# The second feed-forward layer of 28 token blocks as seven quarter products per group of four, with their variance on ScalarE

## The chip, the core and the metric

The kernel runs on one core of a Trainium2 chip. The metric is the device time of one execution in microseconds, from the first to the last instruction. Five engines work side by side, each with its own queue: TensorE (PE in the profile; its weight loads are PEld), VectorE (DVE), ScalarE (ACT), GpSimd (POOL), which here issues the loads of the inputs, and SyncE (SP), which issues the stores and the transposing transfers.

## The reference

The inputs are q, k and v (8 batches, 8 heads, 576 tokens, 64 per head), a gain g of 512 and two weight matrices of 512x2048 and 2048x512, all float32.

```
scores = q k^T / 8, with a bias -slope_h * |i - j|; only 0 <= i - j < 128 is seen
attn   = softmax(scores) v
x      = attn with its heads side by side: (8, 576, 512)
xn     = (x - mean(x)) / sqrt(var(x) + 1e-6) * g
out    = x + relu(xn @ w_ch1) @ w_ch2
```

## The kernel before

**Blocks.** The 4608 tokens are cut into 36 blocks of 128: four pairs of batches, nine blocks each; the ninth (number T = 8 of its pair) holds the last 64 tokens of both batches. The text numbers blocks 0 to 35 in the order of work.

**Attention of a block** is a list of steps written out by hand. From block 8 on there are two to a block. The first (called the *big step* here) takes the masked weights of the block times v into two PSUM tiles `ps_pv` (`values`, L430), divides them on DVE by the sums (L438, L439), centres x to float16 `xc` (`centre`, L459 and L478), lets SP transpose it by DMA into the group's `xT` (L488), computes the scores of the block after next (`scores`, L382, with the exponent on ACT, L390), and in some steps turns the q and k of a later pair of blocks: on PE through two tiles `ps_tr` and copies on DVE and ACT (`turn`, L269, L288 to L294), or for later blocks with a transposing DMA on SP (`turn_natural`, L302). The second (the *mask step*) multiplies the exponents with the decay mask on DVE (L401, two instructions).

**The feed-forward part** works on groups of blocks, `GROUPS = [2] * 4 + [3] * 4 + [4] * 4`. `mlp1(g)` makes the 16 slices of the hidden layer: for each, four matmuls (L636) with a slice of w1 as weights and all columns of the group's `xT` (256, 384 or 512) as the moving operand, then a ReLU to float16, on ACT (L652) or for a few slices on DVE (L644). `mlp2(g)` takes each block by itself: 16 matmuls of 512 columns (L666) with the hidden slice as weights and w2 as the moving operand, all into one PSUM tile, and then one DVE instruction (`finish`, L682) that multiplies with `rstd`, adds x and gives the float32 output, which SP stores with two DMAs (L694, L698). The variance is `bn_stats` and `bn_aggr` on DVE (L503, L504), one block after another in the odd units of `mlp1`, and `inv_std` (L512 to L530) follows for the whole group.

**The order.** `weave_at` (L700) runs the units of `mlp1` or `mlp2` and puts the next attention step behind the units that its list names; -1 is before the first unit. A unit is one slice of `mlp1` (four matmuls) or two matmuls of `mlp2`. PE, ACT and DVE follow the program text exactly, each in order. SP and POOL are ordered by a planner, which goes by its own costs; their queues too are worked off in order. So a matmul stands behind everything that the text puts ahead of it on PE, and a wait of one instruction holds all that follows on its engine.

**PSUM.** The scores have two tiles of two banks each. All else (`ps_m` of both layers, `ps_pv`, `ps_tr`) shares the pool `ps_mm`: four tiles of one bank. A new tile waits until the readers of an old one are done.

The main loop before:

```
            weave_at(mlp2(3), -1, -1, 7, 7)
            for g in range(4, len(GROUPS)):
                in_first = g in (6, 8, 9, 10)
                weave_at(mlp1(g, (9,) * in_first), *(8, 10) * in_first, group=g)
                places = [-1, 7, 15] if g < 8 else [-1, 15, 23] if g < 10 else [-1, 7]
                weave_at(mlp2(g), *2 * places)
```

So in the last groups of three the big steps stand ahead of each block of `mlp2`; in `mlp2(7)`, for instance, those of blocks 22, 23 and 24, while `mlp1(8)` needs blocks 20 to 23.

Of the kernel before, what the change touches and what calls it, by code (L numbers as in the profile page):

```python
# [10 lines left out]
FP16 = mybir.dt.float16  # L11
# [6 lines left out]
P = 128  # L18
# [4 lines left out]
T = 8  # L23
NSLOT = 9
HALF = P // 2
GROUPS = [2] * 4 + [3] * 4 + [4] * 4

NV = 10
AHEAD = 6
# [1 line left out]
FIRST_GROUPS, FIRST = 2, 4  # L31

BY_DMA = SEEN = 8

TURN_BY_DMA = 22

# [23 lines left out]
def kernel(  # L60
# [21 lines left out]
    def pool(name, bufs, **kw):  # L82
        return ctx.enter_context(tc.tile_pool(name=name, bufs=bufs, **kw))
# [30 lines left out]
    def decay(m, at):  # L114
# [340 lines left out]
    def centre(p, blk):  # L455

        total = sums.pop((p, blk))
        mean = small.tile([P, 1], FP32, tag="mean", name="mean")
        nc.vector.tensor_scalar(  # L459
            out=mean,  # L460
            in0=total[:, 0:1],
            scalar1=total[:, 1:2],
            scalar2=1.0 / DM,
            op0=ALU.add,
            op1=ALU.mult,
        )
# [14 lines left out]
        n = p * NSLOT + blk  # L481
        g, at = home[n]
        if at == 0:
            turned_x[g] = group_pool.tile([P, NKB, 4 * P], FP16, tag="xT", name="xT")
        if n < BY_DMA:
            centred[p, blk] = xc
        else:
            nc.sync.dma_start_transpose(  # L488
                out=turned_x[g][:, :, at * P : (at + 1) * P], in_=xc
            )  # L490
# [12 lines left out]
        nc.vector.bn_stats(out=st, in_=xs[order[n]])  # L503
        nc.vector.bn_aggr(out=moments[:, n, :], in_=st)  # L504

    def inv_std(first, n):
# [5 lines left out]
        nc.vector.tensor_scalar(  # L512
            out=aa, in0=moments[:, blocks, 1], scalar1=EPS, scalar2=None, op0=ALU.add
        )
# [51 lines left out]
    def masks_of(n, *halves):  # L566
        return [(masks,) + order[n] + halves]
# [33 lines left out]
    for n in range(8, count):  # L601
        first_half, second_half = values_steps(n)
        step = first_half + second_half
        if n + 1 < count and order[n + 1][1] == T:
            step += [(scores_tail, order[n][0])]
        if n + 2 < count:
            step += scores_step(n + 2)
        if n + 3 < count and order[n + 3][1] % 2 == 0 and not by_dma(*order[n + 3]):
            step += turn_step(n + 3)
        for tag, m in (("k", n + 5), ("q", n + 4)):  # L610
            if m < count and order[m][1] % 2 == 0 and by_dma(*order[m]):
                p, blk = order[m]
# [15 lines left out]
    def mlp1(g, on_dve=()):  # L628
        xT = turned_x[g]
        w = w1 if g < FIRST_GROUPS else w1g  # L630
        cols = len(members[g]) * P
        ht = hidden[g] = hidden_pool.tile([P, NFB, 4 * P], FP16, tag="ht", name="ht")
        for fb in range(NFB):
            ps = ps_mm.tile([P, 4 * P], FP32, tag="mm", name="ps_m1")
            for kb in range(NKB):
# [6 lines left out]
                )  # L642
            if fb in on_dve:
                nc.vector.tensor_scalar(  # L644
                    out=ht[:, fb, 0:cols],
                    in0=ps[:, 0:cols],
                    scalar1=0.0,
                    scalar2=None,
                    op0=ALU.max,
                )  # L650
            else:
                nc.scalar.activation(  # L652
                    out=ht[:, fb, 0:cols], in_=ps[:, 0:cols], func=AF.Relu
                )
            yield cols

    def mlp2(g, parts=((0, NFB),)):
# [3 lines left out]
        for first, end in parts:  # L661
            for at, (p, blk) in enumerate(members[g]):
# [12 lines left out]
                if end == NFB:  # L675
                    finish(p, blk, sums[at])
                    yield DM

    def finish(p, blk, ps):
        n = p * NSLOT + blk  # L680
        o = out_pool.tile([P, DM], FP32, tag="o", name="o")
# [5 lines left out]
            op0=ALU.mult,  # L687
            op1=ALU.add,
        )
        for b, t0, w, p0 in spans(p, blk):  # L690
            dst, src = out[b, t0 : t0 + w, :], o[p0 : p0 + w, :]
            if blk == T:
                last = p == NPAIR - 1 and b % 2 == 1
                (nc.scalar if last else nc.sync).dma_start(out=dst, in_=src)  # L694
# [2 lines left out]
                for r in range(2):  # L697
                    nc.sync.dma_start(out=dst[r], in_=src[r * HALF : (r + 1) * HALF])  # L698

    def weave_at(units, *places, group=None):  # L700


        size = len(members[group]) if group else 0
        first = sum(GROUPS[:group])
# [18 lines left out]
    with tc.manual_schedule(engines={engine.PE}):  # L723
        with tc.manual_schedule(engines={engine.Activation, engine.DVE}):
# [46 lines left out]
```

## Time and profile before

| what | value |
|---|---|
| median of 3 runs | 321.09 us (319.6 to 321.68) |
| the profiled execution's own time | 321.68 us |
| its span | 321.7 us (nothing lies around it) |
| mean granted TensorE clock | 0.994 |
| PE busy | 310.8 us, 97% |
| DVE busy | 198.1 us, 62% |
| ACT busy | 179.4 us, 56% |
| POOL busy | 103.6 us, 32% |
| matmuls of the second layer (L666) | 576, 40% of the chain that ended last |
| matmuls of the first layer (L636) | 768, 40% of that chain |

The profile is of one execution. The chain that ended last is followed back from the last instruction to what released each step. A matmul's duration in the list of groups contains the time of its passage through the array, so a row of matmuls takes less than their number times that duration: what one costs in a row is read from the chain's stretches. Idle time before an instruction is put down to what released it last.

### The profile page before, as it was taken

How to read it: one execution, taken by the hardware profiler on the slowest of the kernel's cores; microseconds unless marked ns; L12 is line 12 of the kernel's file. 1: busy time of each engine (PE TensorE's matmuls, PEld its weight loads, DVE VectorE, ACT ScalarE, POOL GpSimd, SP SyncE). 2: the span in 40 equal slices, each digit the busy share in tenths (PEclk: the TensorE clock that was granted, in tenths of full speed). 3: DMA queues.
4: the chain of work that ended last, by engine and by line, in shares of the span. 5: the costliest groups of instructions: out<-in, count | busy, mean ns of one | idle time of the engine just before them, and what ended most of it. 6: DMA issues, size and time to landing. Idle time of an engine off the chain costs nothing.

```text
span 321.7 us, 9136 instructions
## 1 busy us (share of the span) xinstructions
PE 310.8 (97%) x3806; PEld 177.1 (55%) x3806; DVE 198.1 (62%) x621; ACT 179.4 (56%) x304; POOL 103.6 (32%) x144
## 2 busy tenths in 40 slices
PE   8889999999999999999999989999999999999994
PEld 3478655858656556556556633555455645544441
DVE  2688878787882782877673785437844784516011
ACT  6588756767757557648637634734473457206500
POOL 8933678567311660572680323120000000000000
PEclk9999999999999999999999997999999999999999
DMA  9999999999990993999999599994302320151032
GB/s 117 170 206 195 193 138 192 196 145 140 111 143 0 129 152 51 95 135 153 148 190 141 51 133 144 148 107 91 70 18 43 83 59 19 42 92 33 0 67 65
DMA packets 127260, 35.41 MB, mean 110 GB/s; under 512 B 118385, under 2 KB 122609, under 8 KB 127218
## 3 DMA queue, kind: packets, MB, share of 16 engines
q0 software_dynamic: 92352, 18.36, 72.4%
q1 hardware_dynamic: 34786, 16.33, 29.1%
q8 instruction: 30, 0.49, 0.7%
q14 instruction: 12, 0.10, 0.1%
q10 hardware_dynamic: 80, 0.13, 0.1%
HBM read 36.90 MB, written 9.44 MB: 144 GB/s over the span
## 4 chain that ended last, share of the span: by engine, by line
PE 92%; POOL 2%; DMA 2%; ACT 1%; DVE 1%; issue 1%; POOLq 0%
PE ps_m L666 40%; PE ps_m L636 40%; PE ps_pv L430 5%; PE ps_sc L382 5%; DMA k<-in_k_dram 2%; PE ps_tr L269 2%; POOL q L186 1%; POOL k L186 1%; ACT probs L390 1%; PE ps_sc L269 1%; POOL vx L214 1%; PE ps_tx L498 0%; DVE o L682 0%; ACT k L289 0%; ACT q L288 0%
## 5 line engine op out<-in xcount | busy, mean ns | idle before, releaser
L666 PE MATMUL ps_m<-w,ht 128*128 128x512 f16 x576 | 131.2, 380 | 0.0
L652 ACT ACTIVATE ht<-ps_m 128x384 f16<-128x384 f32 (+2 forms) x183 | 89.8, 491 | 64.7 <-PE ps_m L636 62.0
L636 PE MATMUL ps_m<-xT,w1g 128*128 128x512 f16 (+2 forms) x640 | 116.0, 340 | 2.2 <-DVE st L503 2.2
L636 PEld LDWEIGHTS <-w1g 128*128 128x128 f16 x640 | 62.3, 98 | 52.3 <-issue 4.9
L666 PEld LDWEIGHTS <-ht 128*128 128x128 f16 x576 | 53.4, 98 | 60.7
L390 ACT ACTIVATE probs<-ps_sc 128x1024 f16<-128x1024 f32 x56 | 54.2, 1027 | 43.0 <-PE ps_sc L382 42.8
L682 DVE SCALAR_TENSOR_TENSOR o<-ps_m,rstd,x 128x512 f32<-128x512 f32 x36 | 26.9, 748 | 51.3 <-PE ps_m L666 51.3
L214 POOL DMA_DIRECT2D vx<-in_v_dram x40 | 34.0, 858 | 70.6 <-PE ps_pv L430 41.6
L438 DVE RECIPROCAL rec<-ps_pv 128x4 f32<-128x4 f32 x72 | 12.8, 178 | 44.5 <-PE ps_pv L430 44.4
L401 DVE TENSOR_TENSOR probs<-probs,m 128x1024 f16<-128x1024 f16 x56 | 36.3, 683 | 2.3 <-ACT probs L390 2.1
L439 DVE SCALAR_TENSOR_TENSOR x<-ps_pv,rec 128x256 f16<-128x256 f32 x72 | 30.5, 424 | 2.5
L186 POOL DMA_DIRECT2D q<-in_q_dram x28 | 18.9, 681 | 21.3 <-DMA q<-q 7.8
L503 DVE BATCH_NORM_STATS2 st<-x 128x6 f32<-128x512 f16 x36 | 24.1, 668 | 0.0
L430 PEld LDWEIGHTS <-probs 128*128 128x128 f16 x448 | 18.7, 97 | 6.3 <-DVE probs L401 0.3
L382 PE MATMUL ps_sc<-q,k 64*64 64x128 f16 (+1 forms) x1088 | 19.8, 208 | 1.4 <-ACT probs L390 1.0
L186 POOL DMA_DIRECT2D k<-in_k_dram x28 | 18.6, 676 | 4.9 <-DMA w<-in_moe_w_ch_dram 3.2
L430 PE MATMUL ps_pv<-vx,probs 128*128 128x65 f16 x448 | 20.1, 193 | 0.0
L203 POOL DMA_DIRECT2D q<-in_q_dram x24 | 16.6, 723 | 8.7 <-issue 8.7
L382 PEld LDWEIGHTS <-k 64*64 64x64 f16 x1088 | 14.4, 107 | 6.4 <-issue 4.2
L390 ACT ACTIVATE own<-ps_sc 128x1024 f16<-128x1024 f32 x12 | 11.9, 1030 | 7.3 <-PE ps_sc L382 7.3
L636 PE MATMUL ps_m<-xT,w 128*128 128x256 f16 x128 | 15.0, 273 | 0.0
L636 PEld LDWEIGHTS <-w 128*128 128x128 f16 x128 | 12.1, 98 | 1.3
(59 smaller groups left out, 186.7 us busy)
## 6 DMA issues: line engine op xcount, KB each, us to landing
out_dram<-o SPq DMA_DIRECT2D x71, 128.0 KB, 3.3
k<-in_k_dram POOLq DMA_DIRECT2D x32, 128.0 KB, 6.2
vx<-in_v_dram POOLq DMA_DIRECT2D x32, 128.0 KB, 6.5
w<-in_moe_w_ch_dram POOLq DMA_DIRECT2D x8, 512.0 KB, 10.0
q<-in_q_dram POOLq DMA_DIRECT2D x20, 128.0 KB, 5.6
q<-in_q_dram POOLq DMA_DIRECT2D x32, 64.0 KB, 5.0
k<-in_k_dram POOLq DMA_DIRECT2D x8, 64.0 KB, 4.7
vx<-in_v_dram POOLq DMA_DIRECT2D x8, 64.0 KB, 4.4
```

The costliest lines, as they stand in the source:

```text
L186: nc.gpsimd.dma_start(out=t[b * n // 2 : (b + 1) * n // 2], in_=src[2 * p + b, :, i * P : i * P + n, :].rearrange("h (c r) d -> c h r d", ...
L214: nc.gpsimd.dma_start(out=vx[p0 : p0 + n, :, 0:D], in_=v[b, :, t0 : t0 + n, :].rearrange("h p d -> p h d"),)
L382: nc.tensor.matmul(in_halves(ps[cols, j, n, t, :])[:, r, queries], kt[rows, hp, cols], in_halves(qt[rows, b, hp])[:, r, queries], start=Tr ...
L390: nc.scalar.activation(out=dst.rearrange("p (n j) q -> p j n q", j=2), in_=ps.rearrange("p j n t q -> p j n (t q)"), func=AF.Exp, scale=in ...
L401: nc.vector.tensor_tensor(out=dst, in0=dst, in1=mask, op=ALU.mult)
L430: nc.tensor.matmul(ps[:, i, :], pr[:, h, t, :], vext[(p * NSLOT + o) % NV][:, h, :], start=(n == 0), stop=(n == len(terms) - 1),)
L439: nc.vector.scalar_tensor_tensor(out=xs[p, blk][:, hg * 4 * D : (hg + 1) * 4 * D].rearrange("p (h d) -> p h d", h=4), in0=ps[:, :, 0:D], s ...
L503: nc.vector.bn_stats(out=st, in_=xs[order[n]])
L636: nc.tensor.matmul(ps[:, 0:cols], w[:, kb, fb * P : (fb + 1) * P], xT[:, kb, 0:cols], start=(kb == 0), stop=(kb == NKB - 1),)
L652: nc.scalar.activation(out=ht[:, fb, 0:cols], in_=ps[:, 0:cols], func=AF.Relu)
L666: nc.tensor.matmul(sums[at], ht[:, fb, at * P : (at + 1) * P], w2[:, fb, :], start=(fb == 0), stop=(fb == NFB - 1),)
L682: nc.vector.scalar_tensor_tensor(out=o, in0=ps, scalar=rstd[:, n : n + 1], in1=xs[p, blk], op0=ALU.mult, op1=ALU.add,)
```

## The change

- The last 28 blocks form seven groups of four (blocks 8 to 11, 12 to 15, and so on), where there were four groups of three and four of four.
- For these groups the product of the hidden layer (512 tokens x 2048) with w2 (2048 x 512) is taken in quarters: A11, A12, A21, A22 are 256 tokens x 1024, B11 to B22 are 1024 x 256. Seven products of such quarters (Winograd's form of Strassen's scheme) replace eight. A product is 2 x 8 matmuls with a moving operand of 256 columns (`product`).
- The sums of quarters of w2 (t1 to t4) are made once, by eight DVE instructions in `mlp1(3)` and `mlp2(3)`, in the memory of w1, which only the first two groups use. The sums of quarters of the hidden layer (S1 to S4) are made for each group, by eight DVE instructions of 128x1024 float16: five among the units 5, 9, 12 and 13 of `mlp1`, three at its end.
- The results of the products are added on DVE by `onto`, two instructions of 128x256 for each product, fourteen for a group. Two PSUM tiles go on accumulating: x takes products 1, 3, 5 and 7, and `onto` reads it after each; y takes products 4 and 6; t takes product 2. With P1 to P7 in the order of the text, P3 writes x after `onto` of P1 has read it, P5 after that of P3, P7 after that of P5, and P6 writes y after that of P4.
- Each half row of a block's output is stored by itself: 16 stores for a group in place of 8.
- The variance of these blocks comes from a Square with an accumulated sum on ACT (`square`), in the mask step, in place of `bn_stats` and `bn_aggr`; `inv_std` divides by 512.
- The hidden layer has one buffer (`ht_all`) in place of two.
- `mlp1` of each of the first six of these groups takes a big step at unit 8 and a mask step at unit 10; `mlp2_seven` has 28 units, four to a product, and takes a big step before P1, behind P2 and behind P4, and a mask step behind P1, P3 and P5. The last group takes none. So the big step of the last block that `mlp1(g + 1)` needs stands behind P4 of group g, and that of block 11 still stands in the middle of `mlp2(3)`, where `mlp1(4)` now needs it.

```
--- before.py
+++ after.py
-GROUPS = [2] * 4 + [3] * 4 + [4] * 4
+GROUPS = [2] * 4 + [4] * 7
...
+SEVEN = 4
...
-    xc_pool = pool("xc", 4)
+    xc_pool = pool("xc", 5)
...
-    hidden_pool = pool("hidden", 2)
-    out_pool = pool("outp", 4)
+    out_pool = pool("outp", 5)
+    sums_pool = pool("sums", 1)
...
+    w2sums = w1.rearrange("p kb (n d) -> p (kb n) d", d=DM // 2).rearrange(
+        "p (t fb) d -> p t fb d", t=4
+    )
...
+    ht_all = consts.tile([P, NFB, 4 * P], FP16)
...
-        if n < BY_DMA:
+        if n < BY_DMA or g >= SEVEN:
             centred[p, blk] = xc
-        else:
+        if n >= BY_DMA:
             nc.sync.dma_start_transpose(
                 out=turned_x[g][:, :, at * P : (at + 1) * P], in_=xc
             )
...
+    def square(n):
+        junk = sums_pool.tile([P, DM], FP16, tag="junk", name="junk")
+        nc.scalar.activation(
+            out=junk,
+            in_=centred.pop(order[n]),
+            func=AF.Square,
+            accum_out=moments[:, n, 1:2],
+        )
...
-        steps.append([m for t in (n + 1, n + 2) if t < count for m in masks_of(t)])
+        step = [m for t in (n + 1, n + 2) if t < count for m in masks_of(t)]
+        steps.append(step + [(square, n)] * (home[n][0] >= SEVEN))
...
-        ht = hidden[g] = hidden_pool.tile([P, NFB, 4 * P], FP16, tag="ht", name="ht")
+        at = g % 2 * cols if len(members[g]) == 2 else 0
+        ht = hidden[g] = ht_all[:, :, at : at + cols]
...
+    half = NFB // 2
+    left, right = slice(0, DM // 2), slice(DM // 2, DM)
+    b11, b12 = w2[:, 0:half, left], w2[:, 0:half, right]
+    b21, b22 = w2[:, half:NFB, left], w2[:, half:NFB, right]
+    t1, t2, t3, t4 = (w2sums[:, i] for i in range(4))
+    def minus(out, a, b, op=ALU.subtract):
+        nc.vector.tensor_tensor(out=out, in0=a, in1=b, op=op)
+    def sum_w2(i):
+        c = slice(4 * (i // 4), 4 * (i // 4) + 4)
+        out, a, b = [(t1, b12, b11), (t3, b22, b12), (t2, b22, t1), (t4, b21, t2)][i % 4]
+        minus(out[:, c], a[:, c], b[:, c])
+    hsums = {}
+    def sum_hidden(g, i, c):
+        ht = hidden[g]
+        mid = ht.shape[2] // 2
+        a11, a21 = ht[:, 0:half, 0:mid], ht[:, 0:half, mid:]
+        a12, a22 = ht[:, half:NFB, 0:mid], ht[:, half:NFB, mid:]
+        if (g, i) not in hsums:
+            hsums[g, i] = sums_pool.tile([P, half, mid], FP16, tag=f"s{i}", name=f"s{i}")
+        s = hsums[g, i]
+        c = slice(4 * c, 4 * c + 4)
+        if i == 1:
+            minus(s[:, c], a21[:, c], a22[:, c], ALU.add)
+        elif i == 2:
+            minus(s[:, c], hsums[g, 1][:, c], a11[:, c])
+        elif i == 3:
+            minus(s[:, c], a11[:, c], a21[:, c])
+        else:
+            minus(s[:, c], a12[:, c], hsums[g, 2][:, c])
+    def mlp2_seven(g):
+        ht = hidden[g]
+        s = [hsums.pop((g, i)) for i in (1, 2, 3, 4)]
+        a11, a12, a22 = ht[:, 0:half], ht[:, half:NFB], ht[:, half:NFB]
+        def product(ps, lhs, off, rhs, first):
+            for pair in range(2):
+                at = off + pair * P
+                for fb in range(half):
+                    nc.tensor.matmul(
+                        ps[:, pair, :],
+                        lhs[:, fb, at : at + P],
+                        rhs[:, fb, :],
+                        start=(first and pair == 0 and fb == 0),
+                        stop=(fb == half - 1),
+                        skip_group_check=True,
+                    )
+                    if fb % 4 == 3 and not (pair == 1 and fb == half - 1):
+                        yield
+        def onto(ps, blocks, cols, o=None):
+            fresh = o is None
+            if fresh:
+                o = out_pool.tile([P, 2, DM // 2], FP32, tag="o", name="o")
+            for pair in range(2):
+                p, blk = members[g][2 * blocks + pair]
+                n = p * NSLOT + blk
+                nc.vector.scalar_tensor_tensor(
+                    out=o[:, pair],
+                    in0=ps[:, pair],
+                    scalar=rstd[:, n : n + 1],
+                    in1=xs[p, blk][:, cols] if fresh else o[:, pair],
+                    op0=ALU.mult,
+                    op1=ALU.add,
+                )
+            return o
+        def leave(o, blocks, cols):
+            for pair in range(2):
+                store(*members[g][2 * blocks + pair], o[:, pair], cols)
+        def bank2():
+            t = ps_mm.tile([P, DM], FP32, tag="mm", name="ps_s")
+            return t.rearrange("p (r d) -> p r d", r=2)
+        top, low = 0, 1
+        x = bank2()
+        yield from product(x, a11, 0, b11, True)
+        o11 = onto(x, top, left)
+        yield
+        t = bank2()
+        yield from product(t, a12, 0, b21, True)
+        onto(t, top, left, o11)
+        leave(o11, top, left)
+        yield
+        yield from product(x, s[1], 0, t2, False)
+        o12 = onto(x, top, right)
+        yield
+        y = bank2()
+        yield from product(y, s[0], 0, t1, True)
+        o22 = onto(y, low, right)
+        yield
+        yield from product(x, s[2], 0, t3, False)
+        onto(x, low, right, o22)
+        leave(o22, low, right)
+        yield
+        yield from product(y, s[3], 0, b22, False)
+        onto(y, top, right, o12)
+        leave(o12, top, right)
+        yield
+        yield from product(x, a22, 2 * P, t4, False)
+        leave(onto(x, low, left), low, left)
+        yield
...
-    def weave_at(units, *places, group=None):
+    def weave_at(units, *places, seven=None, sums=None):
...
-            if u % 2 and u // 2 < size:
-                variance(first + u // 2)
-                if u // 2 == size - 1:
-                    inv_std(first, size)
+            if seven is not None:
+                if u == 1:
+                    blocks = len(members[seven])
+                    inv_std(sum(GROUPS[:seven]), blocks, 1.0 / DM)
+                for i, c in {5: [(3, 0)], 9: [(3, 1)], 12: [(1, 0), (2, 0)], 13: [(4, 0)]}.get(u, []):
+                    sum_hidden(seven, i, c)
+                if u == NFB - 1:
+                    for i in (1, 2, 4):
+                        sum_hidden(seven, i, 1)
+            if sums is not None and u % 4 == 1:
+                sum_w2(sums + u // 4)
             advance_to(done + places.count(u))
...
-            weave_at(mlp1(3, (9, 10, 11)), 8, 12)
-            weave_at(mlp2(3), -1, -1, 7, 7)
+            weave_at(mlp1(3, (9, 10, 11)), 8, 12, sums=0)
+            weave_at(mlp2(3), -1, -1, 7, 7, sums=4)
             for g in range(4, len(GROUPS)):
-                in_first = g in (6, 8, 9, 10)
-                weave_at(mlp1(g, (9,) * in_first), *(8, 10) * in_first, group=g)
-                places = [-1, 7, 15] if g < 8 else [-1, 15, 23] if g < 10 else [-1, 7]
-                weave_at(mlp2(g), *2 * places)
+                ahead = g + 1 < len(GROUPS)
+                weave_at(mlp1(g, (9,) * ahead), *(8, 10) * ahead, seven=g)
+                weave_at(mlp2_seven(g), *[-1, 3, 7, 11, 15, 19] * ahead)
```

More of the change, by code (lines that the diff above doesn't have):

```diff
@@ L504, in variance, with inv_std @@
         nc.vector.bn_aggr(out=moments[:, n, :], in_=st)
-    def inv_std(first, n):
+    def square(n):
[6 more added lines that the diff above has]
+        )
+    def inv_std(first, n, scale=None):
         blocks = slice(first, first + n)
@@ L511, in inv_std @@
         hh = small.tile([P, 4], FP32, tag="hh", name="hh")[:, 0:n]
-        nc.vector.tensor_scalar(
-            out=aa, in0=moments[:, blocks, 1], scalar1=EPS, scalar2=None, op0=ALU.add
-        )
+        if scale is None:
+            nc.vector.tensor_scalar(
+                out=aa, in0=moments[:, blocks, 1], scalar1=EPS, scalar2=None, op0=ALU.add
+            )
+        else:
+            nc.vector.tensor_scalar(
+                out=aa,
+                in0=moments[:, blocks, 1],
+                scalar1=scale,
+                scalar2=EPS,
+                op0=ALU.mult,
+                op1=ALU.add,
+            )
         nc.vector.tensor_scalar(
@@ L644, in mlp1 @@
                 nc.vector.tensor_scalar(
-                    out=ht[:, fb, 0:cols],
+                    out=ht[:, fb, :],
                     in0=ps[:, 0:cols],
@@ L652, in mlp1 @@
                 nc.scalar.activation(
-                    out=ht[:, fb, 0:cols], in_=ps[:, 0:cols], func=AF.Relu
+                    out=ht[:, fb, :], in_=ps[:, 0:cols], func=AF.Relu
                 )
@@ new lines @@
+    hsums = {}
[14 more added lines that the diff above has]
+            minus(s[:, c], a11[:, c], a21[:, c])
+        else:
+            minus(s[:, c], a12[:, c], hsums[g, 2][:, c])
@@ new lines, in mlp2_seven @@
+    def mlp2_seven(g):
[13 more added lines that the diff above has]
+                        skip_group_check=True,
+                    )
+                    if fb % 4 == 3 and not (pair == 1 and fb == half - 1):
[12 more added lines that the diff above has]
+                    in1=xs[p, blk][:, cols] if fresh else o[:, pair],
+                    op0=ALU.mult,
+                    op1=ALU.add,
+                )
+            return o
[33 more added lines that the diff above has]
+        yield
@@ L689, in finish, with store @@
         )
+        store(p, blk, o)
+    def store(p, blk, o, cols=slice(0, DM)):
         for b, t0, w, p0 in spans(p, blk):
-            dst, src = out[b, t0 : t0 + w, :], o[p0 : p0 + w, :]
+            dst, src = out[b, t0 : t0 + w, cols], o[p0 : p0 + w, :]
             if blk == T:
@@ L698, in finish @@
                     nc.sync.dma_start(out=dst[r], in_=src[r * HALF : (r + 1) * HALF])
-    def weave_at(units, *places, group=None):
-        size = len(members[group]) if group else 0
-        first = sum(GROUPS[:group])
+    def weave_at(units, *places, seven=None, sums=None):
         advance_to(done + places.count(-1))
         for u, _ in enumerate(units):
-            if u % 2 and u // 2 < size:
-                variance(first + u // 2)
-                if u // 2 == size - 1:
-                    inv_std(first, size)
+            if seven is not None:
[9 more added lines that the diff above has]
+                sum_w2(sums + u // 4)
             advance_to(done + places.count(u))
```

## The prediction

> **What bounds the kernel now.** The page first: busy times and the chain that ended last.
>
> ```profile
> PE 310.8 (97%) x3806; PEld 177.1 (55%) x3806; DVE 198.1 (62%) x621; ACT 179.4 (56%) x304; POOL 103.6 (32%) x144
> ...
> PE 92%; POOL 2%; DMA 2%; ACT 1%; DVE 1%; issue 1%; POOLq 0%
> ```
>
> TensorE is the bound, and after the first 20 us almost without a gap. The second view is that chain in order of time (start, us, what):
>
> ```profile
> 79.71 3.17 PE ps_m L636 x28
> ...
> 88.48 0.46 PE ps_sc L382 x16
> 88.95 3.57 PE ps_m L666 x16
> 92.52 10.40 PE ps_m L636 x64
> ...
> 188.00 3.57 PE ps_m L666 x16
> ...
> 193.72 9.62 PE ps_m L636 x36
> ...
> 289.65 13.81 PE ps_m L636 x64
> 303.46 13.83 PE ps_m L666 x64
> ```
>
> A matmul of 512 columns costs 13.81/64 = 0.216 us in a row, one of 384 costs 0.1625, one of 256 costs 0.109 (28 in 3.17, less the 0.11 by which sixteen of 512 exceed 16 x 0.216 when they begin after other work). Half the columns is half the price: the weight load of each is covered. The one hole stands at the start of `mlp1(8)`: 191.57 to 193.72, and after it 36 matmuls take 9.62 instead of 7.77. The waits and the stretch after the hole (PE, PEld, DVE, ACT and POOL busy, PEclk, DMA share, GB/s):
>
> ```profile
> PE ps_m L636 <- DVE st L503: 2.2, 1, 2.2
> ```
>
> ```profile
> 194.90:198.40 3.50, 3.50 (x10) 1.22 (x8) 2.44 (x11) 1.57 (x3) 2.55 (x4) 0.51 0.86 110
> ```
>
> The named DVE instruction is a neighbour in time: what landed at 193.62 is the transposed `xT` of block 23, whose `xc` was done at 184.66. So a late `xT` cost 2.15 us of waiting and 1.85 us of half clock. The third view is that transfer, from its issue:
>
> ```profile
> L488 SPq DMA_TRANSPOSE xT<-xc x28: 1188/1275/1859, 74.4 to 281.1; - x28
> ...
> DMA to landing us min/median/max: 2.4/4.6/8.1
> ```
>
> Cut to windows: 4.6 for block 11, 5.6 for block 15, 8.1 for 23, 2.4 for most after 225 us, when the loads have ended. Last, the rows of DVE that I price with:
>
> ```profile
> L401 DVE TENSOR_TENSOR probs<-probs,m 128x1024 f16<-128x1024 f16 x56 | 36.3, 683 | 2.3 <-ACT probs L390 2.1
> L439 DVE SCALAR_TENSOR_TENSOR x<-ps_pv,rec 128x256 f16<-128x256 f32 x72 | 30.5, 424 | 2.5
> L682 DVE SCALAR_TENSOR_TENSOR o<-ps_m,rstd,x 128x512 f32<-128x512 f32 x36 | 26.9, 748 | 51.3 <-PE ps_m L666 51.3
> L503 DVE BATCH_NORM_STATS2 st<-x 128x6 f32<-128x512 f16 x36 | 24.1, 668 | 0.0
> ```
>
> **TensorE's own work.** Removed: 28 x 16 = 448 matmuls of 512, 448 x 0.216 = 96.8 us. Added: 7 x 7 x 16 = 784 of 256, 784 x 0.109 = 85.5. That is -11.3. The first layer: 256 of 384 and 256 of 512 (41.6 + 55.3) become 448 of 512 (96.8), -0.1. The hole of block 23 is taken out whole, -4.0, and late `xT` are counted anew below. The end: 4.39 us now lie between the last matmul and the end. After the change two `onto` (0.84) replace one `finish` (0.75), and SP issues three half stores, 0.47 to 0.6 each, where it issued one: +0.3. Base: 321.7 - 11.3 - 0.1 - 4.0 + 0.3 = 306.6 us.
>
> **DVE in the product phase.** Per group leave: four variances, 3.3 us (192.27 to 195.58), and four `finish`, 3.0. Come: eight sums like L401, some 0.65 each in a row, 5.2; fourteen `onto` like L439, 0.42 each, 5.9. So +4.8 or so, to about 26 us in a group of about 30 (four big steps 7.0, four mask steps 5.2, `inv_std` 2.1, a ReLU 0.7 beside the two above). That alone would be cover enough, but it is bunched. From the end of `mlp1` to the end of P7, DVE has three sums (1.95), three big steps (rec to `xc` 1.75 each), three mask steps (1.29 each) and fourteen `onto` (5.9): 17 us. TensorE has 7 x 1.75 + 3 x 0.95 = 15.1. And it is bound to DVE by x and y. The queue of one group without `turn` on PE, in us after the last matmul of `mlp1`; the last ReLU (0.60) ends at 0.65, a `ps_pv` pair with its scores takes 0.95:
>
> ```
> DVE: sums 0.65-2.60 | big 2.60-4.35 | onto P1 -5.19 | mask -6.48 | onto P2 -7.32
>      big -9.07 | onto P3 -9.91 | mask -11.20 | onto P4 -12.04 | big -13.79 (xc)
>      onto P5 -14.63 | mask -15.92 | onto P6 -16.76 | onto P7 -17.60
> PE:  big 0-0.95 | P1 -2.70 | P2 -4.45 | big -5.40 | P3 -7.15
>      P4 7.32-9.07 (its tile y: t is free at 7.32) | big -10.02 | P5 -11.77
>      P6 12.04-13.79 (onto P4) | P7 14.63-16.38 (onto P5)
> ```
>
> 16.38 against 15.10: +1.3 for a group. Where a big step also turns q and k on PE, two more of the four `ps_mm` tiles are wanted while x, t or y are held: `turn` waits until DVE has read t and the `ps_pv`. Behind P2 that is 7.32 and 7.9, so P3 starts at 8.2 instead of 5.4; behind P4 it is 12.6 and 13.2, so P5 starts at 13.5 instead of 10.0. Worked to the end: the group of blocks 8 to 11 (a turn at both places) +3.7, that of 16 to 19 (one behind P4) +3.4. Sum: 3.7 + 3.4 + 4 x 1.3 = 12.3; the last group has no attention and no such wait (P1 and P2 cover the sums). Bounds: 0 if DVE's order leaves cover that I don't see; 18 if each of the some 25 instructions of the phase takes 0.04 more, the gap between L438's end and L439's start in this trace, +1 a group. The Squares on ACT (near L652's 0.60, four to a group, 2.4) lie beside ReLUs and exponents, 17 us of 30: nothing; `inv_std` waits for the last of them, done before P7. The one buffer of the hidden layer costs nothing either: PE reads group g to its end before it makes the first slice of g + 1. The eight sums of w2 stand where DVE waits 0.94 for block 6's last matmul: nothing, or up to 0.7 on block 11.
>
> **Late `xT`.** `mlp1(4)` used to need blocks 8 to 10. Now it needs block 11: `xc` ready at 90.55, landed at 95.25, against 92.5: +2.75, the surest term. In the later groups the last block's `xc` is ready at 13.79 above and P7 ends at 16.38: a lead of 2.6, where block 23 had 6.9. While loads run a transpose needs 5.6: the next `mlp1` waits to 19.4, +3.0 (block 19). After a `turn`, where P7 is late already, +0.65 (blocks 15 and 23). Block 27 (4.9): +2.3. Block 31 (2.4): 0. Block 35 (2.4 to 3.8): +0.7, as no scores follow it. Sum 10.1. Bounds: 3 (block 11 alone) and 20 (8.1 instead of 5.6 for three blocks, and SP behind: blocks 18 and 19 were issued 4.7 and 3.3 us after their `xc`, behind q and k transposes; the stores, now 16 of 0.55 to a group, stand in that queue too).
>
> **Half clock.** Three of these waits (blocks 11, 19, 27) are longer than the 2.15 that was followed by half clock. I take half of them, at 1.85: +2.8; bounds 0 and six, 11. The Trainium skill, page TensorE: Matmul & The Clock Gate, section "What's actually happening", has the clock fall after at least one idle window of about 3.4 us. By that no wait of my list would be long enough and the sum would be 329.0; this trace differs, with a clock of 0.51 after 2.15 us of idling.
>
> **The sum.** 306.6 + 12.3 + 10.1 + 2.8 = 331.8: I predict 332 us, 3.2% above the 321.7 of the profile, 3.4% above the median of 321.09.
>
> **Rivals.**
> 1. *The removed columns win.* If DVE keeps up (the table's lateness falls under half, 6) and transposes land in 2.4 to 4 us, as they do after 225 us, so that only block 11 waits: 306.6 + 6 + 2.75 = 315.4; with a lateness of 2, 311. For it: DVE's total of 26 us in 30 fits, and each `onto` has one product as cover. Against it: 17 us against 15.1 between `mlp1` and P7, and loads run to 216 us.
> 2. *Even.* The same with 2 or 3 waits of 3 us and one half clock: 318 to 324. It lies between.
> 3. *SP's queue becomes the bound.* In the groups of blocks 16 to 27 SP has, per 30 us, 16 stores (8.8), four x transposes (5.1) and some eight q and k transposes (10): 24 us, in order, with waits for loads and DVE. If x transposes are issued 5 us late, as around block 18, three waits grow by 5 and each brings half clock: 332 + 15 + 3 = 350. For it: block 24's transpose was issued 10.9 us after its `xc`. Against it: a stalled TensorE also slows what fills the queue.
> 4. *The change does not remove what it says:* a matmul of 256 with weights from the sums at a price over 0.109, say the 0.1625 of 384 columns: 784 x 0.053 = 42 us more. The 256-wide rows of `mlp1` have a fresh weight for each too, so I give this 0.01 within the third.
>
> **Chances and range.** Forecast 0.58 (324.5 to 342), first rival 0.23 (308 to 318), second 0.11, third 0.08. A difference of 1% is about what this measurement can tell from none. Faster 0.23, same 0.11, slower 0.66. The range 311 to 343 leaves out the slow rival (0.08), the lower part of the fast one (0.07) and little of the forecast.
>
> **What would show it.** PE busy falls by some 11 us less what the clock adds. The list of waits gets PE `ps_m` at L636 on something of SP or a neighbour, once for most groups, the first at about 92.5 for 2.75 us; PE `ps_s` waits on DVE `o`, about 1 us a group; `ps_tr` waits on DVE in three places. DVE rises to about 235 us (198.1 + 7 x 4.8 + eight sums of w2). The granted clock dips after the first of them. The last group takes 26.0 us from its first matmul to its last, instead of 27.6: if that is not so, the price of 256 columns was wrong. I am wrong if TensorE runs through the starts of `mlp1`: then transposes were faster than 5.6 us, or the planner put them ahead on SP.

## The result, and the profile after

| | before | after |
|---|---|---|
| median | 321.07 us (319.6 to 321.68, 4 runs) | 343.47 us (341.89 to 346.04, 4 runs) |
| ratio after / before | | 1.069, 95% interval 1.064 to 1.074 |
| span of the profiled execution | 321.7 us | 342.2 us |
| mean granted clock in it | 0.994 | 0.975 |

The change makes the kernel 6.9% slower. I had forecast 332 us, with a range of 311 to 343: the sign was right, the size too small, and the time lies half a microsecond above the range.

Runs that took over 1.5% more than the fastest of the same kernel are called slow and stay out of the times and ratios: two of the four of experiment 3 (340.7 and 343.33 us) and two of the four of experiment 5 (329.42 and 332.57).

One number of the table ahead of the prediction has to be read anew. The runs from here on have both a time and a span, and the time is 1.7 to 2.4 us above the span. Seven runs of the kernel before with a time of 320.0 to 321.6 have spans of 318.3 to 319.8. By that the execution shown of it, with a span of 321.7, was some 2 us slower than its median; I had set its time equal to its span.

The profile of the changed kernel: busy times, the granted clock in 40 slices of 8.6 us, and the shares of the chain that ended last:

```profile
PE 304.9 (89%) x4078; PEld 204.4 (60%) x4078; DVE 236.2 (69%) x692; ACT 193.3 (56%) x342; POOL 103.4 (30%) x144
...
PEclk9999999999999999999859999999899999999998
...
PE 64%; DVE 20%; DMA 5%; ACT 3%; issue 3%; POOL 2%; SPq 1%; DVEq 0%; POOLq 0%
```

TensorE has 5.9 us less of busy time, though its clock was low for a while, and yet the span is 20.5 us longer: TensorE's busy share fell from 97% to 89%. DVE's 236.2 is what was forecast (235), and its share of the chain went from 1% to 20%. Who TensorE waited for (us in total, times, longest):

```profile
PE ps_m L668 <- DMA xT<-xc: 15.0, 4, 9.7
PE ps_tr L278 <- DVE rec L447: 3.5, 3, 2.3
PE ps_pv L439 <- DVE own L410: 2.8, 3, 1.4
PE ps_tr L278 <- DVE o L778: 1.9, 1, 1.9
PE ps_s L759 <- DVE x L448: 1.8, 1, 1.8
...
PE ps_s L759 <- DVE o L778: 1.0, 3, 0.6
```

The first line is the transposed x at the starts of the first layer, the others are DVE and the PSUM tiles in the product phases (a product phase runs from the last matmul of a group's `mlp1` to the end of its P7). The 9.7 us stand ahead of `mlp1` of blocks 16 to 19. The chain in order of time (start, us, what) there:

```profile
157.77 5.37 PE ps_s L759 x48
...
165.83 1.18 SPq L497
...
167.18 1.25 SPq L311
...
168.52 1.22 SPq L311
...
169.83 2.73 DMA xT<-xc
...
172.81 10.79 PE ps_m L668 x36
```

The last product ends at 163.1. Block 18's `xc` was ready at 155.39 and block 19's at 159.96, but their transposes are issued at 165.74 and 169.83. The clock is at half for 10.24 us, from 168.4, inside the wait, to 178.6, and the first 36 matmuls take 10.79 us instead of 7.77. SP's queue over the stretch (start, us, engine, line, what):

```profile
150.22 1.19 SPq L497 DMA_TRANSPOSE xT<-xc  x1
151.59 3.80 SPq L311 DMA_TRANSPOSE k<-k  x2
155.52 1.23 SPq L311 DMA_TRANSPOSE q<-q  x1
156.93 2.63 SPq L311 DMA_TRANSPOSE k<-k  x2
159.66 1.21 SPq L311 DMA_TRANSPOSE q<-q  x1
160.96 3.28 SPq L847 DMA_DIRECT2D out_dram<-o  x4
164.34 1.30 SPq L311 DMA_TRANSPOSE q<-q  x1
165.74 1.27 SPq L497 DMA_TRANSPOSE xT<-xc  x1
167.18 2.56 SPq L311 DMA_TRANSPOSE k<-k  x2
169.83 1.22 SPq L497 DMA_TRANSPOSE xT<-xc  x1
```

Between block 17's transpose and block 18's the planner has put seven transposes of q and k and four stores, which keep SP busy from 151.6 to 165.7; two more stand ahead of block 19's. In the program text two transposes of q and k and the four stores stand between block 17's and block 18's, and two more transposes ahead of block 19's: four transposes of q and k instead of nine.

### The profile page after: what moved, and what is told of

Same layout as the page of the kernel before. It is cut to its first block, busy times and chain, and to the rows that moved or that the text cites. A ratio compares the mean times of both kernels' runs of the same rounds, so it can differ in the third digit from the quotient of the medians.

```text
span 342.2 us, 9923 instructions
## 1 busy us (share of the span) xinstructions
PE 304.9 (89%) x4078; PEld 204.4 (60%) x4078; DVE 236.2 (69%) x692; ACT 193.3 (56%) x342; POOL 103.4 (30%) x144
## 4 chain that ended last, share of the span: by engine, by line
PE 64%; DVE 20%; DMA 5%; ACT 3%; issue 3%; POOL 2%; SPq 1%; DVEq 0%; POOLq 0%
PE ps_m L668 37%; PE ps_s L759 14%; PE ps_m L698 6%; DVE o L778 4%; DMA xT<-xc 4%; DVE x L448 4%; DVE s L718 3%; DVE probs L410 3%; PE ps_pv L439 3%; PE ps_sc L391 2%; DMA k<-in_k_dram 2%; PE ps_tr L278 1%; ACT probs L399 1%; ACT ht_all L684 1%; DVE rec L447 1%
## 5 line engine op out<-in xcount | busy, mean ns | idle before, releaser
L668 PE MATMUL ps_m<-xT,w1g 128*128 128x512 f16 (+1 forms) x576 | 119.2, 365 | 15.9 <-DMA xT<-xc 15.0
L684 ACT ACTIVATE ht_all<-ps_m 128x512 f16<-128x512 f32 (+1 forms) x165 | 85.8, 521 | 71.1 <-PE ps_m L668 68.5
L399 ACT ACTIVATE probs<-ps_sc 128x1024 f16<-128x1024 f32 x56 | 54.2, 1027 | 18.9 <-PE ps_sc L391 18.9
L759 PE MATMUL ps_s<-w,s 128*128 128x256 f16 x448 | 51.6, 273 | 0.5 <-DVE o L778 0.4
L718 DVE TENSOR_TENSOR s<-ht_all 128x1024 f16<-128x1024 f16 x28 | 19.3, 689 | 43.6 <-ACT ht_all L684 43.5
L759 PEld LDWEIGHTS <-s 128*128 128x128 f16 x448 | 42.9, 98 | 6.7 <-issue 1.2
L759 PE MATMUL ps_s<-w,ht_all 128*128 128x256 f16 x336 | 39.0, 273 | 2.4 <-DVE x L448 1.8
L759 PEld LDWEIGHTS <-ht_all 128*128 128x128 f16 x336 | 32.3, 98 | 7.0 <-DVE x L448 1.9
L698 PE MATMUL ps_m<-w,ht_all 128*128 128x512 f16 x128 | 30.8, 380 | 0.0
L778 DVE SCALAR_TENSOR_TENSOR o<-ps_s,rstd,x 128x256 f32<-128x256 f32 x56 | 24.4, 478 | 7.0 <-PE ps_s L759 7.0
L778 DVE SCALAR_TENSOR_TENSOR o<-ps_s,rstd,o 128x256 f32<-128x256 f32 x42 | 18.3, 478 | 4.9 <-PE ps_s L759 4.8
L212 POOL DMA_DIRECT2D q<-in_q_dram x24 | 16.5, 705 | 16.2 <-issue 11.8
## 6 DMA issues: line engine op xcount, KB each, us to landing
w<-in_moe_w_ch_dram POOLq DMA_DIRECT2D x8, 512.0 KB, 10.4
```

The source lines that it names most:

```text
L399: nc.scalar.activation(out=dst.rearrange("p (n j) q -> p j n q", j=2), in_=ps.rearrange("p j n t q -> p j n (t q)"), func=AF.Exp, scale=in ...
L668: nc.tensor.matmul(ps[:, 0:cols], w[:, kb, fb * P : (fb + 1) * P], xT[:, kb, 0:cols], start=(kb == 0), stop=(kb == NKB - 1),)
L684: nc.scalar.activation(out=ht[:, fb, :], in_=ps[:, 0:cols], func=AF.Relu)
L698: nc.tensor.matmul(sums[at], ht[:, fb, at * P : (at + 1) * P], w2[:, fb, :], start=(fb == 0), stop=(fb == NFB - 1),)
L718: nc.vector.tensor_tensor(out=out, in0=a, in1=b, op=op)
L759: nc.tensor.matmul(ps[:, pair, :], lhs[:, fb, at : at + P], rhs[:, fb, :], start=(first and pair == 0 and fb == 0), stop=(fb == half - 1), ...
```

## The experiments

**Theory.** What was lost is three things: xT that comes late at the group starts (15.0 us, by the regrouping, because the last block is centred later and held up on SP), half clock behind such waits (4.9), and a product phase that runs at DVE's pace (12). **Rivals.** The seven products themselves are the loss; DVE's total is the bound; the loads are late and SP's order only follows.

**1. The regrouping alone.**

```
-                weave_at(mlp2_seven(g), *[-1, 3, 7, 11, 15, 19] * ahead)
+                weave_at(mlp2(g), *[-1, 4, 9, 14, 19, 23] * ahead)
```

with `bn_stats` on DVE in `mlp1` as before, and without the sums of w2 and of the hidden layer.

> The regrouping alone: seven groups of four with the attention steps at the same fractions of the second layer as in the changed kernel, but the second layer as before (64 matmuls of 512 columns to a group) and the variance on DVE as before. Theory (late xT is a cost of the regrouping, the waits on DVE one of the seven products): no wait of PE in the second layer; waits for xT at the start of the first layer of blocks 8 to 11 (about 1.8 us) and 16 to 19 (3 to 9), small ones elsewhere; before without its hole 317.6, plus 8 to 13 of waiting and 2 to 5 of half clock: 327 to 335. Rival (all that was lost hangs on the seven products and DVE's queue): no waits at the group starts, 317 to 320.

Measured: 343.55 us (341.04 to 344.69), ratio 1.069 (1.064 to 1.074), the same as the whole change. The theory's kind of wait, but more of it than the 8 to 13 us expected, so its number is a miss. TensorE's waits in this kernel:

```profile
PE ps_m L668 <- DMA xT<-xc: 16.3, 3, 12.7
PE ps_m L668 <- DMA out_dram<-o: 1.9, 1, 1.9
```

There is no wait on DVE of over 0.2 us in the second layer. The 1.9 stands at the start of `mlp1` of blocks 12 to 15; the profile names a store that landed then, and the landing of block 15's transpose, issued at 124.19, is not in the trace. The 12.7 stand ahead of blocks 16 to 19 and bring half clock from 165.8 to 179.4. So the whole loss can be had without one Strassen product. The waits for xT are 3 us longer here than in the change (18.2 against 15.0), at as much half clock in all (13.65 us), so the equal times do not show that the products cost nothing; experiments 5 and 6 compare them without such waits.

**2. The seven products without the sums of the hidden layer.**

```
-        s = [hsums.pop((g, i)) for i in (1, 2, 3, 4)]
+        s = [a12, a11, a12, a11]
```

and no call of `sum_hidden`.

> The changed kernel without the sums of the hidden layer (56 DVE instructions left out, the products take plain quarters, so the output is another). Theory: the three sums at the end of the first layer stand ahead of the first big step in DVE's queue, so all of the product phase is 2 us late against DVE; without them DVE has 15 us of work beside 15.1 of PE, and the lateness of the six product phases, 14.3 us in all in the changed kernel, falls to 4 to 8; the waits for xT stay (15 us, 9.7 of them at blocks 16 to 19). 331 to 338 by the clock of the changed kernel's 343.5. Rival (DVE's total is the bound, or its bunching is no matter): at most 2 us less, 341 to 344.

Measured: 338.76 us (337.92 to 339.53), ratio 1.055 (1.052 to 1.059). The six product phases with attention take 20.5, 17.5, 18.9, 16.9, 16.4 and 16.6 us in the changed kernel, 106.8 together, and 18.9, 15.6, 17.3, 15.3, 15.4 and 14.9 here, 97.5: 9.3 less, in line with the theory. But the wait for block 19's xT grew from 9.7 to 15.9 us: the products ended 3.5 us earlier (159.7 against 163.1), and that transpose landed 2.9 us later (175.5 against 172.6). So half of the gain was given back, and the time is 0.8 us above the expectation's upper end.

**3. SP in the order of the text.**

```
-    with tc.manual_schedule(engines={engine.PE}):
+    with tc.manual_schedule(engines={engine.PE, engine.SP}):
```

> The changed kernel with SP in the order of the program text instead of the planner's: each x transpose stands ahead of the q and k transposes that the text has behind it. Theory (the 9.7 us at blocks 16 to 19 come from the ten q and k transposes ahead of block 18's and 19's x transposes on SP): that wait falls to 2 to 4, its three windows of half clock to one or none; other starts within 2 us of the changed kernel: 333 to 339. Rival (the loads themselves are late, SP's order follows them): the wait stays, 342 to 347.

Measured: 334.38 and 336.46 us, ratio 1.045 (1.039 to 1.051), inside the theory's 333 to 339. In the profiled execution, with 334.38 the fastest, block 18's transpose is issued 2.2 us after its `xc` instead of 10.4, block 19's 2.5 instead of 9.9, and the waits are

```profile
PE ps_m L668 <- DMA xT<-xc: 8.0, 3, 4.4
```

The wait at block 19 falls from 9.7 to 4.4 and the half clock behind it from 10.24 to 3.41 us. The rival that the loads decide by themselves falls for that execution. It is not the whole of the late xT either: 8.0 of 15.0 us of waiting are left. (The expectation counts ten transposes of q and k ahead of blocks 18 and 19; the queue shown above has nine.)

**4. The attention one block earlier.**

```
-            weave_at(mlp1(3, (9, 10, 11)), 8, 12, sums=0)
+            weave_at(mlp1(3, (9, 10, 11)), 2, 4, 8, 12, sums=0)
...
-                weave_at(mlp2_seven(g), *[-1, 3, 7, 11, 15, 19] * ahead)
+                places = [-1, 3, 7, 11, 15, 19] if g < 9 else [-1, 3, 7, 11] * ahead
+                weave_at(mlp2_seven(g), *places)
```

> The changed kernel with all attention one block earlier (two more steps in the first layer of blocks 6 and 7, two fewer in the last product phase that has any). Theory: each last block is centred a big step (7 to 8 us) before its group starts, so the waits for xT (1.8 + 9.7 + 2.0 + 1.5) and the half clock behind them (4.9) go, all but what SP's queue holds back by more than 8 us (block 19 was held by 9.9: up to 3 us of waiting); the lateness of the product phases stays at 13 to 15. 323 to 330. Rival (the waits for xT only show slack that DVE or the loads would take anyway): less than 6 us are won, 338 to 343.

Measured: 337.33 us (336.0 to 337.96), ratio 1.050 (1.046 to 1.055): between the two expectations, and a miss for the theory's numbers. The waits for xT at blocks 11, 27 and 31 are gone or below 0.8 us. But block 19's transpose is still issued 6.1 us after its `xc` and lands 6.9 after that, 13.0 in all, and the first layer of its group waits 5.8 us. Earlier centring alone doesn't help where SP's order eats the lead.

**5. Both remedies together.** The edits of 3 and 4.

> The changed kernel with both remedies: all attention one block earlier, and SP in the order of the text. Theory (late xT and its half clock are 15 + 5 of what was lost, and go only when the last block is both centred early and not held on SP): no wait of over 1 us at a group start, the clock at 0.99 or more, the lateness of the product phases still 12 to 15: 322 to 328. Rival (a third limit behind these two, such as the loads or DVE's total): waits at the starts or in the attention steps of over 6 us remain, 330 to 337.

Measured: 324.05 and 326.15 us, ratio 1.011 (1.001 to 1.021). With all four runs the median is 327.78, so this figure is less sure than the others; the profile is of the run of 332.57 us, so the waits here tell the kind, not the sum. The theory's expectation holds: no wait for xT is over 0.25 us any more.

```profile
PE ps_tr L278 <- DVE rec L447: 3.0, 3, 2.3
PE ps_sc L391 <- DMA q<-q: 2.2, 1, 2.2
PE ps_pv L439 <- DVE own L410: 2.0, 3, 1.6
PE ps_s L759 <- DVE x L448: 2.0, 1, 2.0
PE ps_tr L278 <- DVE o L778: 1.9, 1, 1.9
```

What is left is the product phase with DVE and the PSUM tiles, and one wait of 2.2 us for a transposed q.

**6. Eight products under both remedies.** The edits of 1, 3 and 4, with `places` [-1, 4, 9, 14, 19, 23].

> The regrouping with eight products, with both remedies (attention one block earlier, SP in the order of the text). Theory (without late xT nothing of the regrouping is left to pay): 318 to 322, as before. Rival (groups of four as such are slower): 326 or more. The difference to the seven products under the same remedies is the net of the seven products themselves: theory +2 to +6 (11.3 of TensorE's work won, 12 to 15 lost to waits on DVE and PSUM tiles, 1 at the end); if the waits on DVE only fill time that late xT would fill, -8 to -11.

Measured: 321.97 us (321.14 to 323.56, 10 runs), ratio 1.001 (0.998 to 1.004): the regrouping costs nothing once xT is in time. In its profile no wait of TensorE is over 0.9 us behind the warm-up, and the clock stays at full from 6.8 us to the last microseconds. So the seven products, in the order that the change gives the work around them and with its variance on ACT, cost some 3 us net (325.1, the mean of experiment 5's two runs, against 322.0). If the count of matmuls saves the 11.3 of the forecast, some 14 are lost to DVE, the tiles and the stores at the end; that is a remainder, not measured by itself.

**7. The attention moved out of the product phase.** The edits of 3 and 4, and

```
-                weave_at(mlp1(g, (9,) * ahead), *(8, 10) * ahead, seven=g)
+                weave_at(mlp1(g, (9,) * ahead), *(4, 6, 10, 12) * ahead, seven=g)
...
+                places = [-1, 3, 27, 27] if g < 9 else [-1, 3] * ahead
```

> The seven products with both remedies, and with the attention taken out of the product phase: two big steps in the first layer (behind units 4 and 10, mask steps behind 6 and 12), one ahead of P1 (mask behind P1), one behind P7 with its mask step. Theory (the lateness comes of 17 us of DVE work beside 15.1 of PE, and of turn and ps_pv wanting PSUM tiles while x, t and y are held): DVE then has 11.7 us beside 13.2, the waits in the product phases fall from 14 to 0 to 5, and most of the 11.3 us of removed work comes out: 309 to 317. Rival (DVE's or ACT's total, or the first layer's crowding, takes it back): 321 to 328.

Measured: 325.84 us (324.71 to 328.61), ratio 1.015 (1.007 to 1.022): the theory's numbers fail. Its waits:

```profile
PE ps_s L759 <- DVE o L778: 5.2, 5, 1.5
PE ps_s L759 <- DVE x L448: 4.8, 2, 2.5
```

One wait in each of the six groups: in four P3 waits 1.1 to 1.5 us for the `onto` of P1, in two, where a turn stands ahead of P1, P1 waits 2.4 and 2.5 us for its PSUM tile until DVE has read a `ps_pv`. DVE's sum of work in the phase had been cut to 11.7 us by the expectation's count, but three sums and a whole big step still stood ahead of that. So cutting DVE's total in the phase was not enough; that its order is what counts is tried next.

**8. The big step in three pieces, none ahead of P1.** The edits of 3 and 4 in their effect, the earlier lists of places lengthened to match the pieces, and

```
-        step = first_half + second_half
+        steps += [first_half, second_half]
+        step = []
...
+                weave_at(mlp1(g, (9,) * ahead), *(3, 4, 5, 7, 8, 9, 10, 12) * ahead, seven=g)
+                places = [3, 7, 7, 11, 15, 19, 19, 23] if g < 9 else [3, 7, 7, 11] * ahead
+                weave_at(mlp2_seven(g), *places)
```

> The seven products with both remedies, and the big step cut in three (first half of the values; second half and centring; scores and turns), so that DVE never has more than 1.3 us of attention between two onto: in the first layer behind units 3, 4, 5 (mask 7) and 8, 9, 10 (mask 12), in the product phase behind P1, P2, P2 (mask P3) and P4, P5, P5 (mask P6), none ahead of P1. Theory (the lateness is one of order, the three sums and a whole big step ahead of the onto that frees x): put down as a queue, no product waits; a turn behind P2 or P5 waits 0.6 to 0.9 for a PSUM tile in three groups. The product phases lose 0 to 4 in all instead of 12 to 14, so 312 to 318, below both kernels. Rival (DVE's 26 us in 30 can't be packed, it is the bound): 321 to 326, waits of 8 or more left.

Measured: 316.89 us (316.28 to 318.11, 6 runs), ratio 0.986 (0.982 to 0.991): 1.4% faster than before, and 26.6 us faster than the change with the same products, sums and additions. Against eight products under the same two remedies (experiment 6, 321.97) it is 5.1 us faster. Its busy times, and its waits in the product phases:

```profile
PE 300.4 (95%) x4078; PEld 201.7 (64%) x4078; DVE 238.5 (76%) x692; ACT 186.0 (59%) x342; POOL 103.7 (33%) x144
```

```profile
PE ps_tr L278 <- DVE x L448: 1.7, 3, 0.7
...
PE ps_tr L278 <- DVE o L779: 0.7, 2, 0.5
```

The product phases now take 16.2, 14.2, 15.8, 13.9, 15.7 and 13.0 us, with two blocks' attention in each where the change has three. DVE is busier than in the change (238.5 against 236.2) and at 76% of the span, so its total is no bound at this point. What is left are waits of 0.3 to 0.7 us at `turn`, 0.7 to 1.1 in each of three groups, where the queue worked out for the expectation had put 0.6 to 0.9. Three things were changed at once: the big step was cut, one block's attention moved from the product phase to the first layer, and nothing was left ahead of P1. No run tells them apart; experiment 7 shows only that moving whole steps, with one still ahead of P1, won nothing.

**9. The variance back on DVE**, under both remedies.

```
-        steps.append(step + [(square, n)] * (home[n][0] >= SEVEN))
+        steps.append(step)
...
+                if u % 2 and u < 8:
+                    variance(sum(GROUPS[:seven]) + u // 2)
```

with `inv_std` behind unit 7.

> The run with both remedies (325 where undisturbed), with the variance of the 28 blocks back on DVE (statistics of one block in units 1, 3, 5 and 7 of the first layer, no Square on ACT). Theory: DVE gets 3.3 us more for each group where it has two big and mask steps, five sums and inv_std in 15.7 us, some 16.6 then, so the three last sums and all of the product phase come up to 1 us later: 326 to 332. Rival (the first layer has room for it): within 2 us of 325.

Measured: 328.46 us (326.01 to 328.96), ratio 1.021 (1.015 to 1.026), against 1.011 (1.001 to 1.021) of experiment 5: some 3 us slower, at the edge of what the runs tell apart. Its four runs had a granted clock of 0.983 to 0.991 and the two of experiment 5 one of 0.997, so the 3 us may be half clock as well as DVE's work. The Square on ACT is a small gain or none, and no cause of the loss.

**10. The kernel before with SP in the order of the text**, the edit of 3.

> The kernel before with SP in the order of the text and nothing else. Theory (its hole at block 23's xT, 2.15 us and 1.85 of half clock in the profile shown, comes of q and k transposes ahead of it, and the other groups have 7 us or more of lead): the hole goes where a run has it, 317 to 321. Rival (SP's order costs nothing there): within 0.3% of before.

Measured: 319.57 us (318.87 to 321.49, 10 runs), ratio 0.993 (0.989 to 0.997). The hole ahead of blocks 20 to 23 is gone and no wait of over 0.5 us stands behind the warm-up. The same habit of the planner cost the kernel before some 0.7% (0.3 to 1.1).

## Why the prediction had the sign right and was too small

The step that failed is the late xT. The sum has block 19's transpose issued as soon as its `xc` is ready, and 3.0 us of waiting; SP issued it 9.9 us after that, behind transposes of q and k that the planner had put ahead, and TensorE waited 9.7 us. With that went more half clock than forecast, and stores that were still in SP's queue at the end. The span of the changed kernel by the terms of the forecast:

| term | forecast | measured | how measured |
|---|---|---|---|
| product phases late against TensorE's own work | 12.3 | 12.2 | 106.8, less the same phases of experiment 2, cleared of their own waits (94.6) |
| late xT | 10.1 | 15.0 | waits of `ps_m` on xT |
| half clock | 2.8 | 4.9 | 36 matmuls in 10.79 and 9.62 us instead of 7.77 |
| base and the rest | 306.6 | 310.1 | what is left of 342.2 |

- **TensorE's own work.** The price was right: 48 matmuls of 256 columns take 5.37 us in a row, 0.109 each and the 0.11 of a new start; the last group runs 26.4 us where 26.0 was forecast, 0.16 of it a wait.
- **The end.** From the last matmul to the end of the span 6.0 us, not 4.7: +1.3. Six stores of P6's and P7's results stood in SP's queue, 0.55 to 0.8 each, and the last half row is issued at 339.25, 2.2 us after its `onto`. I had counted three stores. The other 2.2 us of the table's last line are not assigned; the six product phases cleared of waits take 94.6 us where I had 91 (15.1 each, the turns and the tail blocks' scores added or taken off), and each change of work on TensorE that costs 0.11 may be part of it; that was not tested.
- **DVE in the product phase.** The sum holds to 0.1 us, but in part by luck. The waits that I had named were not those that came: the four phases with no turn behind P2 or P4 were 1.0 to 1.9 us late where I had written 1.3 (6.1 in all against 5.2). I had put that on products waiting for `onto`, and such waits come to 0.8 us there; the others are a turn ahead of P1 that kept P1 from its tile for 1.8, and two waits of 1.4 and 1.2 on the mask of a tail block (`ps_pv` on `own`), none of which I had seen. The two phases with such turns lost 6.1 where I had 7.1: block 18's turn behind P4 waited 1.0 and 0.35, that of block 17 behind P2 1.9 and 0.2, that of block 26 2.3. And `onto` takes 0.478 us, not 0.424. All waits of TensorE in the six phases add up to 11.1 us.
- **Late xT** is the step that failed in size. For blocks 11, 27 and 31 I had 2.75, 2.3 and 0; measured 1.8, 2.0 and 1.5. Blocks 15, 23 and 35, at 0.65, 0.65 and 0.7 in the sum, did not wait. For block 19 I took 3.0, with the transpose issued as soon as `xc` is there, and measured 9.7: SP held it for 9.9 us. Block 27's was held for 1.6 us too, most of its 2.0 if it had landed as fast. I had such delays in the trace of before (blocks 18, 19 and 24 issued 4.7, 3.3 and 10.9 us late), and had put it into the bounds and the third rival instead of the sum. Experiments 3 and 4 show both halves of the cause, and 5 that together they take it away.
- **Half clock.** It followed two of the four waits, about half as assumed, but lasted three times as long at the long one (10.24 us against 3.41). The 1.8 and 1.5 us waits weren't followed by it. Taking half of the waits was a guess; the last section has what the traces show of it. The Trainium skill, page TensorE: Matmul & The Clock Gate, section "What's actually happening", asks for an idle window of about 3.4 us; here the 9.7 us wait fits that, and the 1.97 us wait at 241.3, followed by 3.41 us at half clock, does not.
- **The first rival** (the removed columns win) was wrong for this order of work and right for another: experiment 8 has the same products at 316.9 us, inside the 308 to 318 that I gave it.
- **The third rival** (SP's queue) was the nearest: its mechanism came at one group start, with one wait grown by 6.7 us instead of three by 5. I had given it 0.08.

## What to carry to other kernels

A change of grouping moves the time at which the last member of a group must be ready: count, for the last member alone, the lead from its last instruction through every queue it passes to the group's first use, and count queues that a planner orders by what it has put ahead elsewhere, not by the text. When accumulators are read out between products, each read-out is on the path: what stands ahead of it on its engine can count more than that engine's total. Here cutting a 1.75 us step into pieces, spreading them and keeping them from in front of the first product was worth some 8 us together, where moving it whole was worth nothing. A saving on the busiest engine may be seen only after the waits around it are gone, so compare it with and without under a schedule that has none.

## What I had not expected of the hardware

A wait of TensorE of 1.97 us was followed by 3.41 us at half clock, one of 2.31 us (the turn at 203.3) was not, and at one of 9.7 us the clock was at half for 10.24 us, 5.8 of them after work had started again. The place of a wait decides as much as its length. The half-clock stretches lie on a grid of 3.41 us: in the changed kernel they begin at 168.4 and 243.5 us, 22 x 3.41 apart, and in experiments 1 and 2 the long ones last 13.65 and 17.07 us, four and five times 3.41. Inside the grid step from 240.1 to 243.5 TensorE idled 1.97 us, and half clock followed. The 2.31 us fell on two steps, 1.55 and 0.76, and in experiment 2 a wait of 3.45 us fell on two, 1.76 and 1.69; neither was followed by half clock. With all twelve traces laid out so, between the warm-up and the last matmul, each of the 13 steps at full clock with 1.97 us or more of idling was followed by half clock; those with up to 1.92 were not, but for two (1.67 in experiment 4, 1.50 in experiment 5) that also held many 64x64 matmuls of `turn`. So a wait of 2 us can cost 1.85 us more or nothing.

A transpose of x landed 2.4 to 4.2 us after its issue in blocks 28 to 34, when the loads had ended (at 237.6 us), and 2.5 to 5.9 us before that in the same trace. The Square with its accumulated sum takes 0.63 us on ACT and 0.19 more for reading the accumulator. `scalar_tensor_tensor` with a float32 result of 256 columns and a second tensor of its own takes 0.478 us; the one with a float16 result that divides by the sums takes 0.425.
